# Attention block for one core: x lands transposed by DMA, key maxima scale |Q| in the first head group, and every VectorE exponential takes three VectorE operations

## The chip, the core and the metric

The kernel runs on one core of one Trainium2 chip. A core has TensorE (PE, matrix products into PSUM), VectorE (DVE), ScalarE (ACT), GpSimd (POOL), SyncE (SP, which issues transfers) and 16 DMA engines. The metric is device time in microseconds (us) of one execution; lower is better. The kernel before took 419.52 us (median of three runs, 419.14 to 420.73).

## The reference

One attention block with 16 heads of width 28, for 2048 positions and a model width of 448, in bf16:

```python
qkv = (x @ wqkv).reshape(B, S, 3, H, Dh)            # B=1, S=2048, D=448, H=16, Dh=28
scores = einsum("bhqd,bhkd->bhqk", q, k) * Dh ** -0.5
p = softmax(scores)
o = einsum("bhqk,bhkd->bhqd", p, v)
out = o.reshape(B, S, D) @ wo
```

No score matrix is kept: scores are made tile by tile, exponentiated and multiplied with V at once.

## The kernel before, in words

**Tiles and windows.** The 16 heads form four head groups of four heads. A head is padded from 28 to 32 partitions, so a group's Q or K fills 128. The 2048 queries are four chunks of 512. A window is one head group with one query chunk; there are 16. In a window the keys go by in 16 blocks of 128, so that each window has 16 x 4 = 64 score tiles of 128 keys x 512 queries, 1024 tiles in all. A tile is one matmul (`emit_S`, L652); a row is the four tiles of one key block, and once all four are exponentiated, four matmuls add their products with V to the bank PO (`pv_op`, L816). V has columns of ones, so the softmax denominator comes out beside the product.

**No true maximum is subtracted.** Each head takes 32 more contraction rows beside its own: in Q they hold |Q|, in K a bound made of the largest |K| per dimension (`KMAX`) and a constant mask (`maskm`, -1.03 in data rows, 0 elsewhere). The score matmul over 64 rows thus gives the score less an upper bound. `task_kmax` (L417) makes the bound: four absolute maxima, one per key chunk, are reduced to KMAX, which multiplies the mask; for the first group the first key chunk's rows are written by VectorE (L443) and the others by DMA from `NK` (L438). `task_Q` (L461) makes Q and |Q| (a bitwise AND with 0x7FFF: L491 in the first window, L501 after).

**Two ways to an exponential.** ScalarE takes two tiles at a time from a bank pair PA (one ACTIVATE of 128 x 1024, `try_act`, L955). VectorE takes single tiles from PD or PO by a polynomial on the number's bits (`start_tile`, L735): two linear steps p1 and p2 on VectorE (L757, L760), their product on GpSimd (L763), and a last step f on VectorE that writes the weights PTD (L776). In the kernel before, a tile that starts while GpSimd has little queued goes another way: only p1 on VectorE (L744), then three GpSimd operations (L749, L751, L753), then f. Which tiles go where is decided when the program is built.

**Order.** The order of every engine is fixed at build time by a planner written into the kernel. It keeps a modelled clock, gives each operation a duration, a priority, conditions and banks, and walks forward (the loop at L1000 on). ScalarE pairs come first; a VectorE tile is started when a bank is free; projections of K, Q and V for later groups are tasks with due times. Constants such as J0 (rows that must be ready before a window's first PV), RV, O1 and QEA steer it.

**The start.** Four loads on SP's queue bring x (XS, L208), one more WV (L211); WK and WQ come on ScalarE's queue (L210). Eight matmuls on zeros (L306) run meanwhile. Each block is transposed by 16 TensorE transposes (L322) into PSUM and copied to XT, half by VectorE (L330) and half by ScalarE (L332). XT has 112 contraction rows x 4 pieces. Then come K of the first group (L391), its maxima (L396, L421), K's evictions (L399), Q (L477, L485), |Q| and the bound rows, and the first scores.

**The tail.** The last row groups of the last window are done apart: `finish_window` and the code after the planner's loop copy PO (L684), gather the denominators (`den_gather`, L670; L1090), add the last three rows (L1094), take the reciprocal (L1096), spread it (L1103), scale (L1107), multiply with wo (L1083), add and store (L1112 to L1115).

Of the kernel before, what the change touches and what calls it, by code (L numbers as in the profile page):

```python
# [75 lines left out]
def kernel(  # L76
# [10 lines left out]
    CK = D // CC  # L87
# [18 lines left out]
    J0 = 9  # L106
# [13 lines left out]
    QEA = 20  # L120
# [6 lines left out]
    O1 = 20  # L127
    O2 = 10
    OF = 0.4
    RV = 4  # L130
# [9 lines left out]
    XTH = 1.5  # L140
    PTA1 = 0.6

    x2 = x[0]
    out_perm = out[0].rearrange("(p t) d -> p t d", t=NKT)
    x_perm = x2.rearrange("(p t) c -> p t c", t=NKT)
    wq3 = wqkv.rearrange("(cc p) n -> p cc n", p=CK)

# [7 lines left out]
    XT = [[sb([CK, 2, QW], BF16, f"XT{b}_{hf}") for hf in range(2)] for b in range(NQC)]  # L155
# [19 lines left out]
    DG = DV  # L175
    DW = [sb([P, QW], F16, f"DW{i}") for i in range(2)]
# [21 lines left out]
    OUTF = [sb([P, D], BF16, f"OUTF{i}") for i in range(TPC)]  # L198
# [8 lines left out]
    for b in range(NQC):  # L207
        nc.sync.dma_start(out=XS[b][:], in_=x_perm[:, b * TPC:(b + 1) * TPC, :])  # L208
    for (W, off) in ((WK, D), (WQ, 0)):
        nc.scalar.dma_start(out=W[:, :, 0:GW], in_=wq3[:, :, off:off + GW])  # L210
    nc.sync.dma_start(out=WV[:], in_=wq3[:, :, 2 * D:3 * D])  # L211
# [7 lines left out]

    nc.vector.memset(zeros[:], 0.0)  # L220
# [9 lines left out]
    for i in range(HG):  # L230
        nc.gpsimd.affine_select(out=sel[:, i:i + 1], in_=sel[:, i:i + 1], compare_op=ALU.not_equal,
                                fill=1.0, base=-(HP * i + Dh), pattern=[[0, 1]], channel_multiplier=1)
    nc.gpsimd.memset(ident32[:], 0.0)
    nc.gpsimd.affine_select(out=ident32[:], in_=ident32[:], compare_op=ALU.not_equal,
                            fill=1.0, base=0, pattern=[[-1, P]], channel_multiplier=1)
    for g in range(G):
        for W in (WKP, WQP):
            nc.vector.memset(W[g][:].rearrange("p c (h e) -> p (c h) e", e=HP)[:, :, Dh:HP], 0.0)
    nc.vector.tensor_scalar(out=offscol[:], in0=onescol[:], scalar1=YTOP, scalar2=None, op0=ALU.mult)
# [3 lines left out]
    for g in range(G):  # L243
        nc.vector.memset(VA[g][:].rearrange("p j h e -> p (j h) e")[:, :, Dh:HP], 1.0)
    nc.vector.memset(WO[:], 0.0)
# [55 lines left out]
    xt_half = {}  # L301
# [10 lines left out]
    for b in range(NQC):  # L312
        xs_in = add(Op("SP", 0.01, None, prio=-2000 + b, lat=(4.7, 6.1, 7.6, 9.0)[b]))
        for hf in range(2):
            tv = banks8[2 * b + hf].bitcast(BF16)

            def tr(b=b, hf=hf, tv=tv):
                for c2 in range(2):
                    for t in range(TPC):
                        k = c2 * TPC + t  # L320
                        cc = hf * 2 + c2
                        nc.tensor.transpose(out=tv[0:CK, k * P:(k + 1) * P],  # L322
                                            in_=XS[b][:, t, cc * CK:(cc + 1) * CK], identity=ident[:])
            tro = add(Op("PE", 0.55, tr, deps=[xs_in], prio=-1200 + 10 * b + hf, lat=PLAT, kind="T",
                         acq=(lambda t: not warm_open.__setitem__(0, False)) if (b, hf) == (NQC - 1, 1) else None))

            def ev(b=b, hf=hf, tv=tv):
                i = tv[0:CK, 0:2 * QW].rearrange("p (c q) -> p c q", c=2)
                if hf == 0:
                    nc.vector.tensor_copy(out=XT[b][hf][:], in_=i)  # L330
                else:
                    nc.scalar.copy(out=XT[b][hf][:], in_=i)  # L332
            evo = add(Op("DVE" if hf == 0 else "ACT", 0.6 if hf == 0 else 0.905, ev, deps=[tro], prio=-1200 + 10 * b + hf))
            xt_done[b].append(evo)
            xt_half[2 * b + hf] = evo
# [3 lines left out]
    wkin = add(Op("SP", 0.01, None, prio=-1999, lat=5.1))  # L339
    wqin = add(Op("SP", 0.01, None, prio=-1998, lat=8.3))  # L340
    wvin = add(Op("SP", 0.01, None, prio=-1997, lat=11.0))
# [3 lines left out]
    for g in range(1, G):  # L345
        for (WP, nm, off) in ((WKP, "k", D), (WQP, "q", 0)):
            def ld(g=g, WP=WP, off=off):
                for cc in range(CC):
                    nc.sync.dma_start(
                        out=WP[g][:, cc, :].rearrange("p (h e) -> p h e", e=HP)[:, :, 0:Dh],  # L350
                        in_=wqkv[cc * CK:(cc + 1) * CK, off + g * GW:off + (g + 1) * GW].rearrange("p (h d) -> p h d", d=Dh))
            first = g == 1 and nm == "k"
            w_ready[(nm, g)] = add(Op("SP", 2.4, ld, deps=[xt_done[NQC - 1][0]], prio=-900 if first else g * 256 - 900 + (nm == "q") * 100,
                                      elig=None if first else (lambda t, g=g, nm=nm: pos[0] >= (30 if nm == "q" and g == 1 else (g - 2) * 256 + 120 + 40 * (nm == "q"))), lat=PLT))
# [20 lines left out]
    k0_bank = [(PD[0][:], 0), (PD[2][:], 2), (PO[:], 3), (PA[1][:, QW:2 * QW], 7)]  # L375

    def task_K(g, sc):
        due = g * 4 * WT - 200 + 36 * sc
        if g == 0:
            task = {"slot": None, "ap": k0_bank[sc][0]}  # L380
            acq = lambda t: xt_half[k0_bank[sc][1]].done(t)
# [7 lines left out]
        def ap():  # L389
            return task["ap"] if "ap" in task else bank(task)[:]  # L390
        ops = chain_mm(CC, lambda cc: nc.tensor.matmul(out=ap(), lhsT=WKP[g][:, cc, :], rhs=XT[sc][cc // 2][:, cc % 2, :],  # L391
                                                       start=(cc == 0), stop=(cc == CC - 1)),
                       xt_done[sc] + [w_ready[("k", g)]], prio, elig, acq)
        cs = slice(sc * QW, (sc + 1) * QW)
        if g == 0:
# [3 lines left out]
            evs = [add(Op("ACT", 0.585, lambda pr=pr: nc.scalar.activation(  # L399
                out=KB[0][pr][:, cs], in_=ap(), func=ACT.Identity, bias=onescol[:, 0:1], scale=1.0),  # L400
                deps=[ops[-1], red], prio=prio + 0.1 * pr, lat=0.17,
                acq=(lambda t: quse and quse[0].end is not None) if sc == NQC - 1 else None)) for pr in range(2 if sc == 0 else 1)]
# [14 lines left out]
    def task_kmax(g):  # L417
# [8 lines left out]
        c0 = 1 if g == 0 else 0  # L426
# [716 lines left out]
```

## Time and profile before

| | us |
|---|---|
| the profiled execution's own time | 419.14 |
| its span, first to last instruction | 417.1 |
| median of the runs (419.14 to 420.73) | 419.52 |
| first 1024-column exponential starts | 16.24 |
| last exponential starts | 402.96 |
| last transfers are issued | 414.07 |

The page gives shares by engine and 40 slices of the span; a view by stretches gives each engine's busy time between two moments; a view of waits says who held whom; and the order of time shows single instructions with their start and duration, with the idle time before them and what ended it in brackets. A busy time can be longer than the spacing of instructions, because the end of one overlaps the beginning of the next. "PEld" is TensorE's weight load. The granted TensorE clock is 0.996 of full speed in this run. Of the DMA engines' time, 14.3% went to the queue of most loads.

### The profile page before, as it was taken

The numbers are of one execution on the slowest core, as the hardware profiler recorded it, in microseconds if no ns is written. First come the engines' busy times: TensorE is split into PE (matmuls) and PEld (weight loads), VectorE is DVE, ScalarE is ACT, GpSimd is POOL, SyncE is SP. The second block draws the span as 40 slices with busy tenths as digits, with TensorE's granted clock in tenths as the row PEclk, the third lists the DMA queues.
The fourth block names the chain that finished last, engine by engine and source line by source line (L and its number), as shares of the span: only waits on it lengthen the run. The fifth ranks groups of instructions, "written<-read, shape, count | busy, mean of one in ns | idle before, by whom it ended". The sixth has DMA issues, their size and how long they took to land.

```text
span 417.1 us, 7580 instructions
## 1 busy us (share of the span) xinstructions
PE 363.9 (87%) x2657; PEld 126.1 (30%) x2657; DVE 377.8 (91%) x659; ACT 397.8 (95%) x437; POOL 319.0 (76%) x325
## 2 busy tenths in 40 slices
PE   8989889898988889897988989898888889888996
PEld 5432232222323232322323222322322222222333
DVE  6799999989899999989999999998999899999853
ACT  4999999999999999999999999999999999999961
POOL 3288788797888787798788877888888989787730
PEclk9999999999999999999999999999999999999998
DMA  8410020200401020100401010000311000010112
GB/s 260 73 17 20 3 55 2 48 8 25 100 8 39 1 56 19 29 12 9 114 2 45 3 46 21 7 21 2 96 28 46 2 18 30 9 38 2 70 46 90
DMA packets 33413, 15.84 MB, mean 38 GB/s; under 512 B 26016, under 2 KB 30304, under 8 KB 33376
## 3 DMA queue, kind: packets, MB, share of 16 engines
q1 hardware_dynamic: 32304, 15.05, 14.3%
q8 instruction: 21, 0.34, 0.4%
q10 hardware_dynamic: 1072, 0.32, 0.3%
q14 instruction: 16, 0.13, 0.1%
HBM read 7.37 MB, written 1.96 MB: 22 GB/s over the span
## 4 chain that ended last, share of the span: by engine, by line
ACT 80%; PE 10%; issue 6%; DMA 1%; DVE 1%; SPq 0%; DVEq 0%; ACTq 0%
ACT PTA_132 L955 5%; ACT PTA_131 L955 4%; ACT PTA_133 L955 4%; ACT PTA_136 L955 4%; ACT PTA_137 L955 4%; ACT PTA_140 L955 4%; ACT PTA_138 L955 4%; ACT PTA_134 L955 3%; ACT PTA_139 L955 3%; ACT PTA_141 L955 3%; ACT PTA_142 L955 3%; ACT PTA_143 L955 3%; ACT PTA_135 L955 3%; ACT PTA_144 L955 3%; ACT PTA_145 L955 3%
## 5 line engine op out<-in xcount | busy, mean ns | idle before, releaser
L652 PEld LDWEIGHTS <-KB_1_94 64*128 64x128 bf16 x256 | 21.0, 93 | 50.1 <-issue 48.7
L652 PEld LDWEIGHTS <-KB_1_92 64*128 64x128 bf16 x256 | 20.6, 93 | 47.3 <-issue 44.5
L652 PEld LDWEIGHTS <-KB_0_93 64*128 64x128 bf16 x256 | 20.2, 93 | 43.4 <-issue 41.9
L652 PEld LDWEIGHTS <-KB_0_91 64*128 64x128 bf16 x256 | 19.9, 93 | 40.6 <-issue 37.6
L763 POOL TENSOR_TENSOR DV_180<-DV_180,DU_174 128x512 f16<-128x512 f16 x24 | 27.7, 1153 | 4.5 <-DVE DV_180 L760 3.7
L763 POOL TENSOR_TENSOR DV_177<-DV_177,DU_171 128x512 f16<-128x512 f16 x24 | 27.7, 1155 | 4.0 <-DVE DV_177 L760 3.6
L763 POOL TENSOR_TENSOR DV_179<-DV_179,DU_173 128x512 f16<-128x512 f16 x21 | 24.2, 1155 | 5.6 <-DVE DV_179 L760 4.9
L763 POOL TENSOR_TENSOR DV_176<-DV_176,DU_170 128x512 f16<-128x512 f16 x21 | 24.2, 1154 | 2.1 <-DVE DV_176 L760 1.0
L763 POOL TENSOR_TENSOR DV_175<-DV_175,DU_169 128x512 f16<-128x512 f16 x18 | 20.8, 1153 | 4.0 <-DVE DV_175 L760 3.5
L763 POOL TENSOR_TENSOR DV_178<-DV_178,DU_172 128x512 f16<-128x512 f16 x18 | 20.8, 1155 | 3.2 <-DVE DV_178 L760 2.8
L955 ACT ACTIVATE PTA_139<-PA_195 128x1024 bf16<-128x1024 f32 x18 | 22.4, 1246 | 0.0
L955 ACT ACTIVATE PTA_140<-PA_196 128x1024 bf16<-128x1024 f32 x18 | 22.2, 1233 | 0.2 <-PE PO L816 0.2
L955 ACT ACTIVATE PTA_141<-PA_195 128x1024 bf16<-128x1024 f32 x18 | 22.2, 1236 | 0.0
L955 ACT ACTIVATE PTA_142<-PA_196 128x1024 bf16<-128x1024 f32 x17 | 21.3, 1252 | 0.0
L955 ACT ACTIVATE PTA_138<-PA_196 128x1024 bf16<-128x1024 f32 x17 | 21.1, 1240 | 0.0
L955 ACT ACTIVATE PTA_143<-PA_195 128x1024 bf16<-128x1024 f32 x16 | 20.1, 1254 | 0.0
L955 ACT ACTIVATE PTA_137<-PA_195 128x1024 bf16<-128x1024 f32 x16 | 19.7, 1232 | 0.0
L955 ACT ACTIVATE PTA_136<-PA_196 128x1024 bf16<-128x1024 f32 x15 | 18.5, 1231 | 0.0
L757 DVE TENSOR_SCALAR DU_171<-PD_199 128x512 f16<-128x512 uint16 x24 | 16.4, 683 | 1.7 <-PE PD_199 L652 1.4
L760 DVE SCALAR_TENSOR_TENSOR DV_177<-PD_199,DU_171 128x512 f16<-128x512 uint16 x24 | 16.4, 683 | 0.3
L757 DVE TENSOR_SCALAR DU_174<-PD_199 128x512 f16<-128x512 uint16 x23 | 15.7, 681 | 1.0 <-PE PD_199 L652 0.9
L955 ACT ACTIVATE PTA_146<-PA_196 128x1024 bf16<-128x1024 f32 x13 | 16.4, 1260 | 0.0
(656 smaller groups left out, 1665.8 us busy)
## 6 DMA issues: line engine op xcount, KB each, us to landing
RRB_191<-SCR_193 SPq DMA_DIRECT2D x8, 256.0 KB
RRB_192<-SCR_194 SPq DMA_DIRECT2D x7, 256.0 KB
KB_1_94<-KB_0_93 SPq DMA_DIRECT2D x4, 128.0 KB
XS_127<-in_x_dram SPq DMA_DIRECT2D x1, 448.0 KB
XS_128<-in_x_dram SPq DMA_DIRECT2D x1, 448.0 KB
XS_129<-in_x_dram SPq DMA_DIRECT2D x1, 448.0 KB
XS_130<-in_x_dram SPq DMA_DIRECT2D x1, 448.0 KB
out_dram<-XS_127 SPq DMA_DIRECT2D x1, 448.0 KB
```

The costliest lines, as they stand in the source:

```text
L652: nc.tensor.matmul(out=ap, lhsT=KB[g % 2][i // 2][a:a + 64, j * P:(j + 1) * P], rhs=QB[w % NQB][i // 2][a:a + 64, :], start=True, stop=Tru ...
L757: p1 = add(Op("DVE", P1, lambda: nc.vector.tensor_scalar(out=DU[b][:], in0=lo, scalar1=SIG / 65536, scalar2=SIG * (SS - 0.5), op0=ALU.mult ...
L760: p2 = add(Op("DVE", P1, lambda: nc.vector.scalar_tensor_tensor(out=DV[b][:], in0=lo, scalar=65536 * (SS - 0.5 + CE / C3), in1=DU[b][:], o ...
L763: gq = add(Op("POOL", PTT, lambda: nc.gpsimd.tensor_tensor(out=DG[b][:], in0=DV[b][:], in1=DU[b][:], op=ALU.mult), deps=[p2], prio=n, kind ...
L955: nc.scalar.activation(out=PTA[pslot.idx][:, 0:len(ns) * QW], in_=PA[s.idx][:, 0:len(ns) * QW], func=ACT.Exp, bias=ACT_BIAS, scale=ACT_SCALE)
```

## The change

1. x is no longer loaded as it is and transposed by TensorE. Eight transposing DMAs on ScalarE's queue (two for each block of 512 positions: columns 0 to 383, and the last 128 columns) write XT as 128 contraction rows x 4 pieces. The fourth piece begins at column 320, so 64 of its rows repeat columns that piece three has; the weights of those rows are set to zero (`DUP`). XT's copies and the 64 TensorE transposes are gone. WK, WQ and WV come on SP's queue, each in two loads. The planner's assumed landing times change with it (`XLAND`, `WLAND`).
2. In the first head group the roles of bound and |Q| change places: |Q| is multiplied by KMAX, and K's bound rows are the constant mask, which doesn't wait for the maxima. The first two key chunks' rows are written by GpSimd, the others by DMA from `maskm`. In the first window one of the four |Q| parts is made by ScalarE (Abs with a scale), the others by AND and multiply on VectorE; in the group's later windows GpSimd multiplies. K's third and fourth evictions go from ScalarE to VectorE.
3. The tile way with one step on VectorE and three on GpSimd is gone: each VectorE tile takes p1, p2 and f. GpSimd's product gets a tile of its own (`DG`) in place of writing over `DV`.
4. The position of x's rows in a block is by stretches of 128 rather than interleaved by 16, in the loads and in the output. Some memsets move to GpSimd. J0, QEA, O1 and RV get other values, and the banks of the first projections are assigned anew.

The lists of instructions of the two programs: 1024 score tiles are 843 for ScalarE and 181 for VectorE before (126 with two first steps on VectorE, 55 with one), 848 and 176 after. VectorE has 661 instructions before and 700 after, GpSimd 330 and 231. In the list after, the waits of the transposing loads show that loads share eight completion counters in turn, so that later loads are issued only when the counter's earlier one has landed: the second load of block two waits for WK's first load, block three for WK's second and WQ's first, block four for block one's second and WQ's second.

```diff
-    J0 = 9
+    J0 = 10
...
-    QEA = 20
+    QEA = 30
...
-    O1 = 20
+    O1 = 30
...
-    RV = 4
+    RV = 2
...
+    XLAND = (4.9, 6.6, 8.4, 10.2)
+    WLAND = (4.9, 5.5, 10.5)
...
-        nc.sync.dma_start(out=XS[b][:], in_=x_perm[:, b * TPC:(b + 1) * TPC, :])
-    for (W, off) in ((WK, D), (WQ, 0)):
-        nc.scalar.dma_start(out=W[:, :, 0:GW], in_=wq3[:, :, off:off + GW])
-    nc.sync.dma_start(out=WV[:], in_=wq3[:, :, 2 * D:3 * D])
...
+            nc.scalar.dma_start_transpose(out=XT[b][:, 0:CC - 1, :], in_=xb[:, 0:(CC - 1) * P])
+            nc.scalar.dma_start_transpose(out=XT[b][:, CC - 1:CC, :], in_=xb[:, CS[CC - 1]:D])
+    for (W, off, n) in ((WK, D, GW), (WQ, 0, GW), (WV, 2 * D, D)):
+        for ps, cs, i in w_chunks(off, n):
+            nc.sync.dma_start(out=W[ps, cs, 0:n], in_=i)
...
+    for W in (WK, WQ, WV):
+        nc.vector.memset(W[0:DUP, CC - 1, :], 0.0)
...
-        xs_in = add(Op("SP", 0.01, None, prio=-2000 + b, lat=(4.7, 6.1, 7.6, 9.0)[b]))
+        xs_in = add(Op("SP", 0.01, None, prio=-2000 + b, lat=XLAND[b]))
+        if b not in PEB:
+            xt_done[b].append(xs_in)
+            continue
...
-                kmrep[(g, 0, i)] = add(Op("DVE", 0.36, (lambda i=i, st=st: nc.vector.tensor_scalar(
-                    out=KB[0][i // 2][HP * st:HP * (st + 1), 0:QW], in0=maskm[HP * SI[i]:HP * (SI[i] + 1), :],
-                    scalar1=KMAX[g][HP * SI[i]:HP * (SI[i] + 1), 0:1], scalar2=None, op0=ALU.mult)),
...
+                for c in range(KD):
+                    kmrep[(g, c, i)] = add(Op("POOL", 0.6, (lambda i=i, st=st, c=c: nc.gpsimd.tensor_scalar(
+                        out=KB[0][i // 2][HP * st:HP * (st + 1), c * QW:(c + 1) * QW], in0=maskm[HP * st:HP * (st + 1), :],
+                        scalar1=1.0, scalar2=0.0, op0=ALU.mult, op1=ALU.add)), deps=[kev[(0, c, i)]], prio=-900 + i + 4 * c))
...
+                if i == 1:
+                    o = add(Op("ACT", 0.5, lambda o_=o_, i_=i_, k_=k_: nc.scalar.activation(out=o_, in_=i_, func=ACT.Abs, scale=k_),
+                               deps=[e0, kmax_op[0]], prio=-1090))
...
+                    o = add(Op("DVE", 0.33, lambda o_=o_, k_=k_: nc.vector.tensor_scalar(
+                        out=o_, in0=o_, scalar1=k_, scalar2=None, op0=ALU.mult), deps=[ab, kmax_op[0]], prio=-939 + 0.01 * i))
...
+        if g == 0:
+            ab = add(Op("POOL", PTS, lambda: nc.gpsimd.tensor_scalar(
+                out=QP[n][:], in0=QP[n][:], scalar1=KMAX[g][:, 0:1], scalar2=None, op0=ALU.mult),
+                deps=[ab, kmax_op[0]], prio=-10, kind="n"))
...
-        two = pool_load(t) < XTH and x_busy[0] < t
-        if two:
-            p1 = add(Op("DVE", P1, lambda: nc.vector.tensor_scalar(
...
-            ga = add(Op("POOL", PTA1, lambda: nc.gpsimd.tensor_scalar(
...
-            gb_ = add(Op("POOL", PTT, lambda: nc.gpsimd.tensor_tensor(out=DV[b][:], in0=DU[b][:], in1=DU[b][:], op=ALU.mult),
...
-            gq = add(Op("POOL", PTT, lambda: nc.gpsimd.tensor_tensor(out=DG[b][:], in0=DV[b][:], in1=wb[:], op=ALU.mult),
```

## The prediction, made before the changed kernel was run

> **What bounds the kernel now.** I read the page's shares first, then its 40 slices, then ScalarE's waits, then stretches of the span, and last both ends in order of time. From the page:
>
> ```profile
> PE 363.9 (87%) x2657; PEld 126.1 (30%) x2657; DVE 377.8 (91%) x659; ACT 397.8 (95%) x437; POOL 319.0 (76%) x325
> ...
> ACT  4999999999999999999999999999999999999961
> ```
>
> ScalarE (ACT) is filled in every slice but the first and the last two. Busy times by stretch (columns: stretch, length, then each engine's busy time with its count):
>
> ```profile
> 208.00:256.00 48.00, 41.88 (x303) 13.51 (x295) 46.39 (x81) 48.00 (x54) 38.28 (x37) 1.00 0.09 24
> 16.24:403.60 387.36, 340.48 (x2466) 112.26 (x2464) 361.10 (x613) 386.87 (x422) 315.02 (x306) 1.00 0.13 31
> 403.60:417.10 13.50, 8.78 (x93) 5.72 (x89) 5.54 (x12) 1.37 (x3) 0.00 (x0) 0.87 0.20 69
> ```
>
> From 16.24 to 403.60 ScalarE is busy 386.87 of 387.36 us: a gapless stream of 422 exponentials (421 of 1024 columns, one of 512). So the time is four terms: first exponential at 16.24, the stream, a tail of 13.5, and 2.04 around the span (419.14 - 417.10, the profiled execution's own time). The sum is made against 419.14; the median, 419.52, is 0.4 higher. About 0.5% (2.1 us) is what a measurement of this kernel can tell from no change.
>
> VectorE (DVE) matters second: busy 361.10 of 387.36 in the stream, 46.39 of 48 in one stage, and there ScalarE still lost nothing.
>
> **The stream.** By the two programs' instruction lists, 1024 score tiles divide into 843 for ScalarE and 181 for VectorE before, 848 and 176 after. That is 424 exponentials of 1024 columns. Spacing: from 17.50 (the second) to 402.96 (the last) there are 420 steps, 385.46 us, 0.918 each. Before: 16.24 to 403.59 = 387.35. After: 423 x 0.918 + 1.03 for the last + 0.2 that the second waits for VectorE's extra operations = 389.5. **+2.2.**
>
> VectorE's tiles cost more. Before, 126 take three VectorE operations and 55 take two (488); after, 176 x 3 = 528. GpSimd goes from 126 + 55 x 3 operations to 176, so nothing of its part can be late: it sheds 55 x (0.62 + 1.04 + 1.15) = 155 us and gains 50 x 1.155 = 58. A VectorE operation is shown as 0.68 but the next starts 0.60 on:
>
> ```profile
> 204.95 0.68 DVE L776 SCALAR_TENSOR_TENSOR PTD_158<-PD_197,DV_178 128x512 uint16<-128x512 f32 x1
> 205.55 0.68 DVE L776 SCALAR_TENSOR_TENSOR PTD_159<-PD_198,DV_179 128x512 uint16<-128x512 f32 x1
> ```
>
> So 40 x 0.60 = 24.0 more, and two key evictions that ScalarE did (2 x 0.65): 361.1 + 25.3 = 386.4 of a stream of 389.5. The old busy time counts an overlapping 0.08 before each gap; by spacing alone its operations add up to about 353, so after about 378, 97%. Cover is nearly gone. Bounds for what ScalarE then loses: nothing, as in the stage at 46.39 of 48; or, if VectorE keeps the 26 us that it now idles, 386.4 + 26.3 - 389.5 = 23. I take 0.8, near the lower end: the stage at 97% is the closest row, and the exponentials are ordered so that VectorE gets fewer tiles.
>
> **The start.** The order of time, old kernel (start, duration):
>
> ```profile
> 9.29 0.61 PE L322 MATMUL PA_195<-ident,XS_130 128*112 128x128 bf16 x8
> ...
> 12.22 0.59 PE L391 MATMUL PA_196<-XT_0_69,WKP_79 112*128 112x512 bf16 x2
> ...
> 13.36 0.69 DVE L396 TENSOR_REDUCE KPART_95<-PA_196 128x1 f32<-128x512 f32 x1 [0.17 <-PE PA_196 L391]
> 14.08 0.16 DVE L421 TENSOR_REDUCE KMAX_99<-KPART_95 128x1 f32<-128x4 f32 x1
> 14.28 0.72 DVE L443 TENSOR_SCALAR KB_0_91<-maskm,KMAX_99 32x512 bf16<-32x512 bf16 x2
> 15.03 0.60 DVE L491 TENSOR_SCALAR QB_0_85<-QB_0_85 32x512 uint16<-32x512 uint16 x2
> 15.78 0.39 PE L652 MATMUL PA_195<-QB_0_85,KB_0_91 64*128 64x512 bf16 x2
> ```
>
> The last x block is there at 9.07 (its first weight load). Then come 64 transposes' last 16, their evictions on VectorE and ScalarE, the key projection, four maxima, bound rows, |Q|. Transposes and evictions go: 9.07 to 12.22, 3.15 us. After the key maximum the old chain has 0.72 of bound rows and 0.60 of |Q|; in their place stand one multiply on VectorE (0.36, half of L443's pair) and beside it one scaled Abs on ScalarE. That form is not in the trace; between 0.30 (half of L491) and 0.69 (ScalarE's 128x512 eviction) I take 0.69, its own engine. The chain from the landing: four matmuls and their end 12.22 to 13.36 = 1.14; reduction 0.72; maximum 0.20; Abs with its wait 0.10 + 0.69; last score matmul to exponential 0.25 + 0.15 = **3.25** in all. Old: 7.17.
>
> When does the last block land? No row shows a transposing load. Lower bound: as a plain load, 9.07. Upper: each byte holds the DMA engines twice as long; the blocks filled them from about 2.6 to 9.07, so 15.5. Two things speak for more than 9.07. By the list's waits, loads share eight completion counters: the last block's two transposing loads may issue only once the first block's second part and the second part of WQ are there, and WQ was waited for until 8.08 before. And ScalarE's queue holds eight issues ahead of its table load (1.28) and its evictions. The planner in the diff assumes 10.2; of its old assumptions (4.7, 6.1, 7.6, 9.0) the trace shows 4.6, 6.2, 7.85, 9.07. I take 10.4, nearer to the plain load. First exponential: 10.4 + 3.25 = 13.65, **-2.6**. Per us of later landing, +1.
>
> The Trainium skill ("DMA: Bandwidth & Descriptors", Latency and other measured facts) gives a transposing DMA an effective 261 GB/s, or 350-400 when contiguous. This trace moved plain blocks 1.5 us apart (448 KB, about 300 GB/s) and shows no transposing one. An estimate from the page: 1.835 MB at 261 is 7.0 us, 2.0 + 7.0 + 1.6 for the weights = 10.6, and the sum 0.2 higher.
>
> A second rule speaks against the change. The fillers stand 0.43 apart early (3.57 for eight), later matmuls 0.215 (0.86 for four). The skill ("TensorE: Matmul & The Clock Gate", What's actually happening) says the slow clock is the default and comes back after an idle window of about 3.4 us. Without transposes TensorE waits for landings; if it fell slow, the last four matmuls would cost 0.86 more.
>
> Hidden at no cost: memsets moved to GpSimd (VA 0.27 each on VectorE; GpSimd waited 4.39 us for WQ there), constant bound rows (8 GpSimd operations, 0.62 each by L749's row for the same operation on more partitions, and four copies on SP's queue, needed from tile 16 and 32, some 6 and 12 us later), three Q multiplies on GpSimd (0.62 each, 24 us ahead of use). If this cover went, the first windows would wait 1 to 2 us.
>
> **The tail.** Old kernel, last exponential to end:
>
> ```profile
> 402.96 0.63 ACT L955 ACTIVATE PTA_143<-PA_196 128x512 bf16<-128x512 f32 x1
> ...
> 403.85 0.69 DVE L684 COPY OSB_186<-PO 128x512 f32<-128x512 f32 x1 [2.26 <-PE PO L816]
> ...
> 405.13 1.06 PE L670 MATMUL PD_199<-sel,OSB_186 128*128 128x4 f32 x8 [0.65 <-DVE XS_129 L622]
> ...
> 408.25 0.26 DVE L1096 RECIPROCAL RT<-PD_199 128x16 f32<-128x16 f32 x1 [2.11 <-PE PD_199 L1090]
> ```
>
> After its last score matmul (402.23) the old TensorE still had 20 PV matmuls; then copy, additions, the denominators (L670), three rows of L1090 and L1094 (0.82 each), done at 408.7, 5.1 after the last exponential. In the new list all PV but the last three rows stand ahead of the third last score pair, some 3.6 us before the last exponential ends, and L670's matmuls between the last pairs. The old chain from PV's end to 408.7 takes 4.9, so it would end 1.3 to 2.0 after the exponential. Gain between 0 (VectorE, now full, copies late) and 3.7; I take 3.1, nearest to the list's order. Tail 10.4, **-3.1**.
>
> **Sum.** 13.65 + 389.5 + 0.8 + 10.4 + 2.04 = **416.4**, 0.65% under 419.14.
>
> **Rivals.**
> - *VectorE becomes the bound* (the other side). Place: the score stream, where a PV row waits for its VectorE tiles and TensorE, in order, holds back the next score pair. From VectorE waits of about 11 us (389.5 less 378) on, each us is one. If it keeps 19 to 24 of its idle, ScalarE loses 8 to 13: 424 to 429. For: 97%. Against: 96.6% in one stage without loss. Chance 0.16.
> - *Transposing loads are slow.* Last landing at 12 to 15.5: 418 to 421.5. For: the shared counters. Against: bytes are the same. 0.15.
> - *The tail gives nothing* because VectorE is behind at the end: 419.5. 0.08.
> - *The change does less than it says*: blocks land as plain loads would (9.07), and nothing is lost: 414 to 415. 0.06.
> - Forecast, 415 to 417.4: 0.55.
>
> Faster by over 0.5% (under 417.4): forecast, the last rival, a little of the slow loads: 0.62. Within: 0.21. Slower: 0.17, the first rival. Range 413.2 to 421.4: from the earliest landing with the full tail gain to the latest landing; left out is the first rival.
>
> **What would show it.** First exponential at 13 to 15; 424 exponentials of 0.918 with under 2 us of idle; VectorE busy 97-99% of the stream; denominators' reciprocal within 3 us of the last exponential. Wrong if ScalarE waits for score matmuls in mid-stream, or the first exponential is past 16.

## The result: 424.3 us, 1.1% slower, and the whole miss lies before the first exponential

The changed kernel takes 424.34 us (median of four runs, 423.56 to 424.57) beside 419.33 for the kernel before on the same chip (418.52 to 420.73): a ratio of 1.0113, with a 95% interval of 1.0082 to 1.0143 (further down intervals stand in brackets behind the ratio to the kernel before, which ran again beside every run). The forecast was 416.4 with 421.4 as its upper end.

The profiled execution took 424.49, its span is 422.6. From the page after (engines' shares, ScalarE's row of slices, two DMA queues with packets, MB and share of 16 engines; q10 is ScalarE's queue):

```profile
PE 366.6 (87%) x2612; PEld 122.1 (29%) x2612; DVE 393.6 (93%) x698; ACT 396.1 (94%) x435; POOL 237.2 (56%) x226
...
ACT  0499899999999999999999999999999999999991
...
q1 hardware_dynamic: 32576, 13.22, 13.3%
q10 hardware_dynamic: 8592, 2.21, 3.1%
```

ScalarE's first slice went from 4 to 0, its second from 9 to 4; the last but one went from 6 to 9. The view by stretches, cut at the first and last exponential (length, busy times of PE, PEld, DVE, ACT and POOL with counts, granted clock, DMA share, GB/s):

```profile
22.22:412.48 390.26, 347.81 (x2520) 114.03 (x2519) 381.42 (x657) 389.10 (x424) 225.77 (x194) 1.00 0.13 30
412.48:422.60 10.12, 6.15 (x62) 3.87 (x58) 3.83 (x10) 1.37 (x4) 0.00 (x0) 0.83 0.26 91
```

| term | before | forecast | after | after less forecast |
|---|---|---|---|---|
| last x block is there | 9.07 | 10.4 | 18.12 | +7.7 |
| from there to the first exponential | 7.17 | 3.25 | 4.10 | +0.85 |
| stream | 387.36 | 390.3 | 390.26 | 0 |
| tail | 13.50 | 10.4 | 10.12 | -0.3 |
| around the span | 2.04 | 2.04 | 1.89 | -0.15 |

Three of five terms came out to 0.3 us, over 390 us of stream. The start is 8.6 us off. In order of time, ScalarE's queue of the changed kernel (start, duration):

```profile
0.71 1.40 ACTq L226 DMA_TRANSPOSE XT_63<-in_x_dram  x1
...
3.45 2.18 ACTq L226 DMA_TRANSPOSE XT_64<-in_x_dram  x1
5.67 1.52 ACTq L227 DMA_TRANSPOSE XT_64<-in_x_dram  x1
...
11.75 1.68 ACTq L227 DMA_TRANSPOSE XT_66<-in_x_dram  x1
13.46 1.28 ACT L235 ACT_TABLE_LOAD   x1 [13.46 <-DMA XT_65<-in_x_dram]
...
22.22 1.02 ACT L994 ACTIVATE PTA_127<-PA_195 128x1024 bf16<-128x1024 f32 x1 [0.46 <-PE PA_195 L709]
```

Each transposing load holds the queue for 1.28 to 2.18 us, eight of them until 13.43. The plain loads of x before held SP's queue for 0.38 to 0.52 each. TensorE and the chain to the first exponential:

```profile
12.20 0.81 PE L418 MATMUL PO<-XT_65,WKP_75 128*128 128x512 bf16 x3 [1.23 <-DMA XT_65<-in_x_dram]
13.82 0.38 PE L418 MATMUL PO<-XT_65,WKP_75 128*128 128x512 bf16 x1 [0.81 <-DMA XT_65<-in_x_dram]
18.17 1.87 PE L418 MATMUL PD_198<-XT_66,WKP_75 128*128 128x512 bf16 x4 [3.97 <-DMA XT_66<-in_x_dram]
```

The chain of waits has one piece here, "9.96 8.16 DMA XT_66<-in_x_dram": from the issue of block four's first load to its landing. The four products that follow take 1.87 where the forecast's chain had them at a full clock; the clock granted from 18 to 20 us is 0.50. DMA engines are over-full all the while, and a view of the transfers alone, 0 to 20 us, says with what:

```profile
q10 hardware_dynamic: 8448, 2.10, 63.2%
q1 hardware_dynamic: 2104, 1.14, 32.7%
```

63.2% of 20 us is 12.6 us of all 16 engines for 2.10 MB of x, and 32.7% is 6.5 us for 1.14 MB of weights, wo and constant rows. Together 19.1 us. The view by stretches has the engines at a share of 1.19 (last number but one; packets of one engine overlap, so it can be over 1):

```profile
2.00:18.00 16.00, 8.20 (x24) 2.69 (x23) 5.26 (x18) 4.52 (x7) 7.48 (x19) 0.88 1.19 199
```

So 19.1 us of packets fill the 16.1 us from 2 to 18.1, where block four lands. This only adds up what the trace holds; what the parts are worth, runs 2 to 5 show.

### The profile page after: what moved, and what is told of

Read it like the earlier page. It is cut to its first block, busy times and chain, and to the rows that moved or that the text cites. A ratio compares the mean times of both kernels' runs of the same rounds, so it can differ in the third digit from the quotient of the medians.

```text
span 422.6 us, 7570 instructions
## 1 busy us (share of the span) xinstructions
PE 366.6 (87%) x2612; PEld 122.1 (29%) x2612; DVE 393.6 (93%) x698; ACT 396.1 (94%) x435; POOL 237.2 (56%) x226
## 4 chain that ended last, share of the span: by engine, by line
ACT 83%; issue 6%; PE 5%; ACTq 2%; DMA 2%; DVE 0%
ACT PTA_127 L994 4%; ACT PTA_129 L994 4%; ACT PTA_128 L994 4%; ACT PTA_131 L994 4%; ACT PTA_132 L994 4%; ACT PTA_130 L994 4%; ACT PTA_137 L994 4%; ACT PTA_133 L994 4%; ACT PTA_136 L994 4%; ACT PTA_135 L994 4%; ACT PTA_134 L994 4%; ACT PTA_139 L994 3%; ACT PTA_141 L994 3%; ACT PTA_138 L994 3%; ACT PTA_145 L994 3%
## 5 line engine op out<-in xcount | busy, mean ns | idle before, releaser
L805 POOL TENSOR_TENSOR DG_177<-DV_171,DU_165 128x512 f16<-128x512 f16 x30 | 34.7, 1155 | 29.5 <-DVE DV_171 L802 29.4
L805 POOL TENSOR_TENSOR DG_178<-DV_172,DU_166 128x512 f16<-128x512 f16 x30 | 34.6, 1155 | 29.1 <-DVE DV_172 L802 28.9
L805 POOL TENSOR_TENSOR DG_181<-DV_175,DU_169 128x512 f16<-128x512 f16 x29 | 33.5, 1155 | 29.0 <-DVE DV_175 L802 28.2
L805 POOL TENSOR_TENSOR DG_180<-DV_174,DU_168 128x512 f16<-128x512 f16 x29 | 33.5, 1154 | 26.3 <-DVE DV_174 L802 25.8
L805 POOL TENSOR_TENSOR DG_179<-DV_173,DU_167 128x512 f16<-128x512 f16 x29 | 33.5, 1155 | 21.1 <-DVE DV_173 L802 20.9
L805 POOL TENSOR_TENSOR DG_182<-DV_176,DU_170 128x512 f16<-128x512 f16 x29 | 33.5, 1156 | 20.9 <-DVE DV_176 L802 20.7
L994 ACT ACTIVATE PTA_141<-PA_195 128x1024 bf16<-128x1024 f32 x18 | 22.6, 1258 | 0.0
L994 ACT ACTIVATE PTA_140<-PA_196 128x1024 bf16<-128x1024 f32 x18 | 22.6, 1254 | 0.0
L994 ACT ACTIVATE PTA_139<-PA_195 128x1024 bf16<-128x1024 f32 x18 | 22.5, 1251 | 0.0
L994 ACT ACTIVATE PTA_138<-PA_196 128x1024 bf16<-128x1024 f32 x18 | 22.5, 1249 | 0.0
L994 ACT ACTIVATE PTA_136<-PA_196 128x1024 bf16<-128x1024 f32 x18 | 22.4, 1247 | 0.0
L994 ACT ACTIVATE PTA_137<-PA_195 128x1024 bf16<-128x1024 f32 x18 | 22.4, 1246 | 0.0
L994 ACT ACTIVATE PTA_135<-PA_195 128x1024 bf16<-128x1024 f32 x18 | 22.4, 1246 | 0.0
L994 ACT ACTIVATE PTA_134<-PA_196 128x1024 bf16<-128x1024 f32 x18 | 22.4, 1242 | 0.0
L799 DVE TENSOR_SCALAR DU_168<-PD_197 128x512 f16<-128x512 uint16 x29 | 19.7, 679 | 0.8 <-PE PD_197 L709 0.8
L799 DVE TENSOR_SCALAR DU_167<-PD_199 128x512 f16<-128x512 uint16 x29 | 19.7, 681 | 0.7 <-PE PD_199 L709 0.5
L799 DVE TENSOR_SCALAR DU_165<-PD_197 128x512 f16<-128x512 uint16 x29 | 19.7, 681 | 0.6 <-PE PD_197 L709 0.5
L802 DVE SCALAR_TENSOR_TENSOR DV_174<-PD_197,DU_168 128x512 f16<-128x512 uint16 x29 | 19.7, 681 | 0.2
```

The costliest lines, as they stand in the source:

```text
L799: p1 = add(Op("DVE", P1, lambda: nc.vector.tensor_scalar(out=DU[b][:], in0=lo, scalar1=SIG / 65536, scalar2=SIG * (SS - 0.5), op0=ALU.mult ...
L802: p2 = add(Op("DVE", P1, lambda: nc.vector.scalar_tensor_tensor(out=DV[b][:], in0=lo, scalar=65536 * (SS - 0.5 + CE / C3), in1=DU[b][:], o ...
L805: gq = add(Op("POOL", PTT, lambda: nc.gpsimd.tensor_tensor(out=DG[b][:], in0=DV[b][:], in1=DU[b][:], op=ALU.mult), deps=[p2], prio=n, kind ...
L994: nc.scalar.activation(out=PTA[pslot.idx][:, 0:len(ns) * QW], in_=PA[s.idx][:, 0:len(ns) * QW], func=ACT.Exp, bias=ACT_BIAS, scale=ACT_SCALE)
```

## The experiments

Theory A: the loss is the landing of transposed x, and the other parts are worth what was forecast. The rivals are in the texts on record.

**1. All blocks by TensorE (e1).**

```diff
-    PEB = ()
-    XLAND = (4.9, 6.6, 8.4, 10.2)
+    PEB = (0, 1, 2, 3)
+    XLAND = (4.7, 6.1, 7.6, 9.0)
```

(and banks for the four added transposes)

> The changed kernel with part 1 undone: all four x blocks come by plain loads on SP's queue and TensorE transposes them; the other parts stay. Theory A (only the late landing of the transposing loads costs; stream and tail are as predicted): last block at about 9.1, transposes and copies 3.2, then 3.3 to 4.1 to the first exponential, so 15.5 to 16.5 in place of 22.2; stream 390.3, tail 10.2, 1.9 around: 418 to 419. Rival B (the 40 more VectorE operations cost the time): the stream loses in any case, 422 or more. Rival C (ScalarE's queue, not the landing): same first exponential as A.

Measured: 423.17, ratio 1.0092 [1.0061, 1.0123], first exponential at 21.89. The time lies in rival B's range, but not by B's cause, for the stream takes 390.6 as in the changed kernel. Theory A missed by an effect of the undoing itself:

```profile
10.15 0.28 DVE L320 COPY WKP<-WK 128x448 bf16<-128x448 bf16 x1 [5.30 <-DMA WK<-in_wqkv_dram]
10.34 0.68 DVE L358 COPY XT<-PA 128x1024 bf16<-128x1024 bf16 x1
```

WK now stands on SP's queue behind all of x. VectorE waits 5.30 us for it, and the copies of x's transposes, long ready, queue behind that one copy. The weights' queue belongs to part 1, and this run didn't undo it; run 6 does.

**2. Transposing loads on SP's queue, weights on ScalarE's (e2).**

```diff
-            nc.scalar.dma_start_transpose(out=XT[b][:, 0:CC - 1, :], ...
+            nc.sync.dma_start_transpose(out=XT[b][:, 0:CC - 1, :], ...
...
-            nc.sync.dma_start(out=W[ps, cs, 0:n], in_=i)
+            nc.scalar.dma_start(out=W[ps, cs, 0:n], in_=i)
```

> The eight transposing loads are issued by SP, the weights' loads by ScalarE. Theory A (landing): the first exponential stays at 21 to 23 and the time at 423 to 425. Rival C (ScalarE is held by 12.7 us of issues, then its table load and six evictions up to 18.3, and that sets the start): ScalarE is free from 3 us on, the first exponential comes 2 to 6 us earlier, 418 to 422.

Measured: 420.32 (one run), first exponential at 17.80: rival C's range. But the landing moved too, which C did not say. The issues are no faster (1.23 to 2.14 each, the last ends at 13.11), yet block four's products start at 14.54, 3.6 us earlier:

```profile
11.85 1.26 SPq L227 DMA_TRANSPOSE XT<-in_x_dram  x1
13.22 1.80 SPq L270 DMA_DIRECT2D WO<-in_wo_dram  x4
```

```profile
14.54 1.06 PE L418 MATMUL PD<-XT,WKP 128*128 128x512 bf16 x4 [0.92 <-DMA XT<-in_x_dram]
```

WO is issued behind x and no longer shares the engines with it; as x's queue changed as well, run 4 has to separate the two. TensorE runs at its full clock (1.00 from 14 to 15 us; four products 1.06), and the chain from them to the first exponential takes 3.26: the forecast's 3.25 was right for a TensorE at full clock.

**3. A third of the bytes in each block's first load (e3), and two issues in place of eight (e4).** e3 loads 128 columns for 384, and the middle pieces of XT are constants; e4 loads all 2048 rows at once.

```diff
-            nc.scalar.dma_start_transpose(out=XT[b][:, 0:CC - 1, :], in_=xb[:, 0:(CC - 1) * P])
+            nc.scalar.dma_start_transpose(out=XT[b][:, 0:1, :], in_=xb[:, 0:P])
```

> Still eight transposing loads, but each block's first brings 128 columns in place of 384 (half of the transposed bytes); the two middle pieces of XT are set to a constant, so that much of x is left out. Theory A1 (the DMA engines' time on the transposed bytes sets the landing): 13 us of the 16 engines become some 6.5, the last landing falls from 18.1 to 12 to 14, the first exponential to 16 to 18. Rival A2 (the count of issues, 1.3 to 2.2 us each, sets it): last landing stays at 17 to 18.

```diff
-    for b in range(NQC):
+    for k in range(1):
...
+        nc.scalar.dma_start_transpose(out=XTA[k][:, 0:CC - 1, :], in_=xb[:, 0:(CC - 1) * P])
```

> The same transposed bytes in two loads of 2048 rows in place of eight of 512 rows. Theory A1 (engine time on the bytes): the data are all there at 15 to 18, no block earlier. Rival A2 (count of issues): all there by 8 to 10, the first exponential below 15 and the time at 417 or less.

Measured: e3 422.47, e4 427.56 (one run each). With half the bytes each issue still takes 1.24 to 1.40 and the eighth ends at 11.32, though the engines' time on that queue is halved (1.5% of the span for 3.1%). With two issues the queue is held as long:

```profile
0.71 7.93 ACTq L224 DMA_TRANSPOSE XTA<-in_x_dram  x1
8.67 4.49 ACTq L225 DMA_TRANSPOSE XTA<-in_x_dram  x1
13.18 1.28 ACT L233 ACT_TABLE_LOAD   x1 [13.18 <-issue]
```

In both, the last piece of x lands some 3 us earlier than in the changed kernel:

```profile
15.05 0.38 PE L420 MATMUL PD<-XT,WKP 128*128 128x512 bf16 x1 [0.86 <-DMA XT<-in_x_dram]
```

```profile
15.22 0.59 PE L416 MATMUL PA<-XTA,WKP 128*128 128x512 bf16 x1 [0.34 <-DMA XTA<-in_x_dram]
```

e3 (15.05, first exponential 18.03) stands between its two theories. e4 has the same bytes and lands at 15.22, as A1 said, and A2 falls; there WO is issued at 13.48, behind x as in run 2, and the time is long because no block is there before 13.44 (first exponential 22.50). So there are two floors of about the same height: the queue (some 1.3 us for 512 rows however few the columns, about 12.5 us for all of x) and the engines (12.6 us). Neither fewer issues nor fewer bytes alone moves x to 9 us.

**4. WV and WO out of x's way (f1).**

```diff
-    for (W, off, n) in ((WK, D, GW), (WQ, 0, GW), (WV, 2 * D, D)):
+    for (W, off, n) in ((WK, D, GW), (WQ, 0, GW)):
...
+    for ps, cs, i in w_chunks(2 * D, D):
+        nc.scalar.dma_start(out=WV[ps, cs, 0:D], in_=i)
...
+    add(Op("SP", 2.4, ld_wo, prio=-800, elig=at(160), lat=6.0))
```

> The changed kernel with two loads taken out of the way of the transposing loads: WV's two loads follow the transposing loads on ScalarE's queue, and WO's four are issued late in the stream; nothing else is changed but what the plan makes of it. Theory D (the last block lands late because other loads' packets share the 16 DMA engines with it; with the weights' issue on SP and nothing behind it, it landed at about 14.5): the last block's first product is at 14.3 to 15.3 instead of 18.17, the first exponential at 18 to 19, total 420.0 to 421.3. Theory E (ScalarE's queue itself is slow at transposing loads; SP's queue is the better one): the last block is still there only at 17 to 18.5, first exponential 21 to 22.5, total 423 to 425.

Measured: 430.56, ratio 1.0278 [1.0250, 1.0305]. On the landing theory D is right and E falls: block four's products start at 14.09 on ScalarE's queue too. WO is the load that runs 2 and 4 both took out of x's way.

```profile
14.09 1.02 PE L421 MATMUL PD<-XT,WKP 128*128 128x512 bf16 x4 [1.01 <-DMA XT<-in_x_dram]
18.22 1.87 PE L952 MATMUL PD<-zrow,zeros 128*128 128x512 bf16 x4 [3.11 <-ACT QB L527]
```

On the time both miss, D by 9 us, because the edit made new waits. ScalarE's first eviction stands behind ten issues and the table load (15.17), Q's comes at 16.89. |Q| waits for that one, and VectorE's last reduction queues behind |Q|, 3 us after its products:

```profile
17.62 0.53 DVE L540 TENSOR_SCALAR QB<-QB 32x512 uint16<-32x512 uint16 x1 [3.82 <-ACT QB L527]
18.18 0.69 DVE L426 TENSOR_REDUCE KPART<-PD 128x1 f32<-128x512 f32 x1
```

First exponential: 20.69. In run 2, with block four as early and ScalarE free of the issues, it was 17.80: the queue that rival C named costs up to 2.9 us once the landing no longer hides it. TensorE, idle 3.11 us, then runs at half clock (0.50 from 18 to 24), and ScalarE waits before each of the next pairs. WO's late issues on SP at 82.86 hold up Q's copies, and one exponential comes 2.20 late at 99.07:

```profile
22.70 2.06 ACT L997 ACTIVATE PTA<-PA 128x1024 bf16<-128x1024 f32 x2 [0.98 <-PE PA L712]
25.18 1.02 ACT L997 ACTIVATE PTA<-PA 128x1024 bf16<-128x1024 f32 x1 [0.42 <-PE PA L712]
...
99.07 13.86 ACT L997 ACTIVATE PTA<-PA 128x1024 bf16<-128x1024 f32 x15 [2.20 <-PE PA L712]
```

The stream takes 395.0 for 390.3, the tail 11.8.

**5. Plain loads in the transposing loads' place (g1).** Same bytes, tiles and queue:

```diff
-            nc.scalar.dma_start_transpose(out=XT[b][:, 0:CC - 1, :], in_=xb[:, 0:(CC - 1) * P])
-            nc.scalar.dma_start_transpose(out=XT[b][:, CC - 1:CC, :], in_=xb[:, CS[CC - 1]:D])
+            xf = xb.rearrange("(p t) d -> p (t d)", t=TPC)
+            nc.scalar.dma_start(out=XT[b][:, 0:CC - 1, :].rearrange("p c q -> p (c q)"), in_=xf[:, 0:(CC - 1) * QW])
+            nc.scalar.dma_start(out=XT[b][:, CC - 1, :], in_=xf[:, TPC * D - QW:TPC * D])
```

> The changed kernel with its eight transposing loads replaced by eight plain loads of the same bytes (2.10 MB, into the same tiles, on the same queue and with the same waits after them); x is then not transposed, so this run leaves out that part of the computation. Nothing else is changed. Theory A (how long the transposing loads take is the whole error): last block there at 9 to 11, first exponential at 12.5 to 14.5, stream and tail as in the changed kernel (390.3 and 10.1), total 415 to 417.5. Rival F (the weights on SP, the eight issues ahead of ScalarE's evictions, or a slow TensorE clock would hold the start up even so): first exponential after 16, total over 418.5.

Measured: 418.10, ratio 0.9966 [0.9948, 0.9984], between the two theories. Transfers of the first 16 us, and the last x pieces:

```profile
q10 hardware_dynamic: 1152, 2.10, 40.0%
q1 hardware_dynamic: 2104, 1.14, 28.0%
```

```profile
11.42 0.81 PE L419 MATMUL PD<-XT,WKP 128*128 128x512 bf16 x3 [0.73 <-DMA XT<-in_x_dram]
12.82 0.38 PE L419 MATMUL PD<-XT,WKP 128*128 128x512 bf16 x1 [0.59 <-DMA XT<-in_x_dram]
```

The first exponential comes at 15.39, 6.8 us earlier than in the changed kernel, with nothing changed but the kind of load. 40.0% of 16 us is 6.4 us for the same 2.10 MB that took 12.6 transposed. Engine time also depends on what else is in flight: with WO behind them (run 2, first 14.5 us) the transposed bytes took 73.1%, 10.6 us,

```profile
q1 hardware_dynamic: 8449, 2.11, 73.1%
```

and the 1.14 MB of other loads took 4.5 us here (28.0%) for 6.5 beside transposing loads. So transposing takes 1.7 to 2.0 times the engine time of plain loads. But plain loads of this layout, with the weights on SP beside them, also land only at 12.8, not at 9 to 11. So 7.7 us of late landing divide into 5.3 (18.1 - 12.8) for transposing and 2.4 (12.8 - 10.4) that any load in this arrangement would pay: 14% more bytes of x, 1.14 MB of other loads in the same stretch, and issues held until an earlier load has landed (the fourth on ScalarE's queue stands until 4.19). Which of these makes the 2.4 was not tried. Nor is the 5.3 a fixed price: with WV and WO out of the way, transposed x landed at 14.09 (run 4), 1.3 later than the plain loads here.

**6. TensorE transposes with the weights where they were (f2).** As run 1, and WK and WQ on ScalarE's queue:

```diff
-            nc.sync.dma_start(out=W[ps, cs, 0:n], in_=i)
+            (nc.sync if n == D else nc.scalar).dma_start(out=W[ps, cs, 0:n], in_=i)
```

> Part 1 undone with the weights where they were before: all four x blocks come as plain loads on SP and are transposed by TensorE, WK and WQ come on ScalarE's queue, WV on SP behind x. Parts 2, 3 and 4 of the change stay. Theory A (the whole loss is the start, and there the landing of transposed x; bound rows that are constants, three VectorE steps, the new constants and the tail are each worth what was forecast): the first exponential is at 14.8 to 16.2, no later than the 16.24 of before, and the time is 416.3 to 418.3, under before. Rival (the gain of the tail or the three-step tiles needs the new start, or the bound rows gain nothing): 418.5 to 421.

Measured: 419.53, ratio 1.0019 [1.0003, 1.0036]. The landing's loss is gone, but so is the gain: the rival's range. First exponential 16.82, second 18.50 (before: 16.24, 17.50), tail 10.6.

**7. Two blocks transposed by DMA (f3), one block (g4).** f3: blocks one and two plain on SP, three and four transposing on ScalarE's queue. g4: run 6 with block four by two transposing loads on SP behind the plain ones.

```diff
-    PEB = ()
+    PEB = (0, 1)
```

> Blocks one and two of x as plain loads on SP (each followed by WK's, then WQ's loads) and TensorE transposes, blocks three and four by four transposing loads on ScalarE's queue; parts 2, 3 and 4 stay. If the issue of transposing loads (1.3 to 2.2 us each) sets the landing: the four are issued by 6.5, the last block is there at 8 to 10.5 and the first exponential is at 12.5 to 15; total 414.5 to 417. If instead the bytes of transposing loads set it (2.21 MB took 13.1 us of all engines; half of that, 6.5 us, beside 1.2 MB of plain loads at 320 GB/s, 3.7 us): last landing 10.5 to 12, first exponential 14.5 to 16, total 416.5 to 418.5. If plain and transposing loads hinder each other: first exponential after 17, total over 419.

```diff
-    PEB = (0, 1, 2, 3)
+    PEB = (0, 1, 2)
...
-            nc.scalar.dma_start_transpose(out=XT[b][:, 0:CC - 1, :], ...
+            nc.sync.dma_start_transpose(out=XT[b][:, 0:CC - 1, :], ...
```

> The version with all four blocks transposed by TensorE and weights on ScalarE's queue (419.5), but with block four alone by two transposing loads, issued by SP behind the three plain x loads. Theory A with the measured terms (two issues of 1.3 after the plain ones, 0.55 MB at some 170 GB/s behind the plain loads): block four is there at 10.5 to 12 in place of the 14 at which its evicted transposes were; first exponential at 15 to 16 in place of 16.82, second with no gap; total 417 to 418.8. If transposing and plain loads hinder each other as in the mixed version (a plain x block that came 3 us late): first exponential over 16.8, total 419.5 to 421.5.

Measured: f3 423.48, ratio 1.0115 [1.0086, 1.0144]. The third case held: the plain block two came at 9.18 beside the transposing loads (6.2 in the kernel before, where its issue ended 1.4 us earlier, at 1.58 for 3.02), the fourth issue took 3.21, the table load (8.91) and both copies of x on ScalarE (from 10.21) started behind it, and the first exponential came at 19.13.

g4 423.37, ratio 1.0090 [1.0070, 1.0111]. Its first exponential is where theory A said (15.87), the earliest of all versions that transpose x, though the two issues took 2.38 and 2.93 and the second exponential came 0.8 late (17.68). The gain is lost again further on, and theory A's total with it: TensorE's clock is 0.50 from 20 to 24 us, pairs come late there and the stream takes 392.7; and its plan leaves 88 matmuls behind the last exponential (62 in the changed kernel), the reciprocal comes 4.35 after it (1.6), and the tail is 14.3:

```profile
15.87:408.61 392.74, 349.43 (x2497) 113.61 (x2495) 381.85 (x655) 389.52 (x424) 225.34 (x195) 0.99 0.13 30
408.61:422.90 14.29, 9.34 (x88) 5.83 (x86) 5.23 (x12) 1.37 (x3) 0.00 (x0) 0.71 0.18 65
```

**8. Part 3 out of the changed kernel (f4), and part 3 alone in the kernel before (g2).** f4 puts the two-way tile back; g2 takes it out of the old kernel (GpSimd's product still writes over DV there).

```diff
+        two = pool_load(t) < XTH and x_busy[0] < t
+        if two:
```

> The changed kernel with the two-way VectorE tile put back (one VectorE step and three GpSimd steps when GpSimd has little queued, as before); x still lands transposed. If part 3 is worth what was forecast (VectorE full costs 0.8 us over the stream, and the plan with three-step tiles takes five tiles fewer on VectorE): 423.5 to 425.5, no more than 1 us from the changed kernel's 424.3. If three-step tiles cost the stream more than forecast: 420.5 to 423. If they are a gain of their own (less GpSimd work beside VectorE): 425.5 to 428.

```diff
-        two = pool_load(t) < XTH and x_busy[0] < t
-        if two:
```

> Part 3 alone: the kernel before with three VectorE operations for every VectorE tile; start, bound rows and constants stay. If part 3 costs only what the count of ScalarE's exponentials says (424 for 422, two tiles fewer for VectorE in each pair: +2.2 us) and VectorE at 97% costs 0.8, and the tail's gain is not part 3's: 421.5 to 423. If the shorter tail (3 us) comes with the three-step tiles: 418.5 to 420.5.

Measured: f4 430.98, ratio 1.0286 [1.0257, 1.0315]; g2 417.11, ratio 0.9937 [0.9912, 0.9961]. f4 lies beyond the third case expected of it and g2 below its second: part 3 is a gain, in either surrounding. g2 by stretches:

```profile
16.43:405.85 389.42, 345.06 (x2499) 112.70 (x2498) 381.13 (x656) 389.06 (x424) 221.17 (x191) 1.00 0.13 31
405.85:415.40 9.55, 5.34 (x79) 3.48 (x77) 3.90 (x10) 1.37 (x3) 0.00 (x0) 1.00 0.28 98
```

The stream pays 2.06 for three-step tiles (2.2 forecast), with VectorE busy 97.9% and ScalarE idle for 0.36 us in all. The tail gives back 3.95, of which 1.45 lie behind the reciprocal, where the work is the same and the clock is not (last section). f4 has a tail of 14.6 and a stream of 392.0 for two exponentials fewer.

**9. The four constants alone (g3), and with part 3 (h1).**

```diff
-    J0 = 9
+    J0 = 10
-    QEA = 20
+    QEA = 30
-    O1 = 20
+    O1 = 30
-    RV = 4
+    RV = 2
```

> Part 4's four planner constants alone: the kernel before with J0 10, QEA 30, O1 30 and RV 2; tiles, start and bound rows stay. If the shorter tail comes with the constants (the plan then puts the last PV matmuls before the last score pairs, with 423 exponentials in place of 422): 416 to 418. If the tail's gain needs the three-step tiles, as the changed kernel with two-way tiles (tail 14.6) suggests: 419 to 421.

> Parts 3 and 4's constants together on the kernel before: three VectorE operations for every VectorE tile and J0 10, QEA 30, O1 30, RV 2; x, its transposes and the bound rows stay. Beside the version with parts 2, 3 and 4 and no part 1 (419.5, first two exponentials at 16.82 and 18.50), this leaves out only part 2, the 128-row pieces and the order of x's rows. If part 2 is worth nothing at the start or costs (two more VectorE operations between the maximum and the second exponential): first two at 16.2 to 16.5 and 17.5 to 17.8, total 416 to 418. If part 2 gains and the 419.5 comes from parts 3 and 4 together: 419 to 421.

Measured: g3 416.39, ratio 0.9926 [0.9901, 0.9950]; h1 416.96, ratio 0.9941 [0.9917, 0.9964]. Both times are in the first case's range (h1's first two exponentials, at 16.04 and 17.30, even 0.2 earlier than it said), and with g2 these three are faster than either kernel; their intervals overlap, so no order among them is shown. Parts 3 and 4's constants do not add up: each alone brings the reciprocal to within 2.2 or 2.3 us of the last exponential, both to 1.6. Against the kernel before on its own chip h1 is 2.6 us faster (419.52); f2, which has part 2 and the new layout besides, is 0.6 slower (418.96). Between the two profiles (spans of 414.2 and 418.4; h1's execution was 1.0 faster than its median, f2's 0.7 slower) stand 0.8 of start, 1.7 of stream and 1.7 of tail (the last goes with the clock, below):

```profile
16.04:405.25 389.21, 344.98 (x2508) 113.73 (x2517) 380.24 (x657) 388.98 (x424) 221.29 (x191) 1.00 0.13 31
405.25:414.20 8.95, 4.77 (x62) 2.98 (x58) 3.74 (x10) 1.37 (x4) 0.00 (x0) 1.00 0.30 104
```

```profile
16.82:407.78 390.96, 347.96 (x2520) 114.26 (x2518) 382.20 (x658) 389.14 (x424) 225.79 (x195) 1.00 0.12 30
407.78:418.40 10.62, 6.43 (x62) 4.12 (x58) 3.76 (x10) 1.37 (x3) 0.00 (x0) 0.76 0.25 88
```

## Why the prediction was wrong, point by point

- **The landing, the step that failed.** The last x block was forecast at 10.4 and came at 18.12. "Upper: each byte holds the DMA engines twice as long [...] so 15.5" doubled the old stretch from 2.6 to 9.07, and that held too little:

```profile
2.60:9.07 6.47, 6.23 (x58) 3.91 (x56) 4.75 (x12) 2.50 (x4) 2.00 (x7) 1.00 1.05 352
```

  By this row the engines worked 6.8 us there (1.05 of 6.47), on x's 1.84 MB and about 0.5 MB of other loads; doubled, 13.6. In the changed kernel they worked 19.1 us by 18.1: 12.6 on x, which has 14% more bytes (2.10 MB; "bytes are the same" and the 1.835 MB of the estimate leave out the columns that are loaded twice), and 6.5 on 1.14 MB of other loads. The factor two had no row behind it, but came out about right (1.7 to 2.0, run 5). The choice of 10.4, "nearer to the plain load", had no row behind it either: it rested on the planner's assumption, written into the code, and on plain blocks. Even plain loads in this arrangement land at 12.8 (run 5).
- **"ScalarE's queue holds eight issues"** was named, at no price. Each took 1.28 to 2.18 us, and that queue also carries the table load and the evictions. Here it wasn't the last wait, since block four came later still; in run 4 it was.
- **The chain, 3.25.** Measured 4.10, and 3.26 with TensorE at full clock (run 2). The excess is mostly the four last products: 1.90 to the reduction for 1.14, at a clock of 0.50. That case was priced in the text at 0.86, for the clock rule of the Trainium skill ("TensorE: Matmul & The Clock Gate", What's actually happening), and left out of the sum. It came with the late landing: in run 5, where x landed piece by piece until 12.82, the clock was 1.00 throughout. The trace has the slow clock (0.53 from 14 to 16 us, 0.50 from 16 to 20) but not that rule's condition, an idle window of about 3.4 us before it: the clock fell at 14.2, as the 3.97 us without work began, and from 1.60 until then no wait of TensorE had been longer than 1.4 us.
- **Part 2.** From the start of the maximum to the first exponential: 2.16 before (14.08 to 16.24), 1.43 after (20.79 to 22.22), as forecast. In run 6 it was 1.51, but the maximum came 1.2 later there than before (15.31 for 14.08), and the second exponential waits for two more multiplies. Which of the new layout, the split weight loads and the order of evictions makes the maximum late wasn't taken apart. On this kernel parts 1, 2 and the layout together gain nothing.
- **The stream, 390.3.** Right to 0.1. Of the 0.8 allowed for a full VectorE, 1.16 us of idle were seen after the first exponential, but in one place, 46.2 to 48.4 us, where TensorE does PV matmuls of many rows between two score pairs. VectorE at 97.9% of the stream cost nothing in g2. So the first rival fell, and that the allowance had about the right size is luck: what it was meant for cost nothing. VectorE's busy time was 381.42, 5 less than the 386.4 that was added up.
- **The tail, 10.4.** Right, 10.12: the reciprocal is 1.63 after the last exponential ("1.3 to 2.0"). That the sum is within 0.3 is partly luck, since the 8.49 us behind the reciprocal go with the clock, by up to 2.4 us between the runs shown in the last section.
- **The rivals.** "Transposing loads are slow: 418 to 421.5" had the mechanism, at 0.15 and with a bound that was too low. It was this one that ended slower than before, not VectorE.

The Trainium skill ("DMA: Bandwidth & Descriptors", Latency and other measured facts) gave 261 GB/s and, with it, an estimate of 10.6. Here 2.10 MB in 12.6 us of all engines are 167 GB/s (198 with the 10.6 us of run 2), and from the first issue to the last landing (17.4 us) it is 121. A second page ("Advanced Engine Details and Errata", X-Bar Transpose (TRN2)) says that transposing transfers are as fast as regular ones; the changed kernel and run 2, beside run 5, show 1.7 to 2.0 times the engine time. The measurement decides.

## What to carry to other kernels

Before a load is moved into another form, add up the engine time of everything that is in flight in the same stretch, with the new form at its worst bound, and see which queue each issue holds and who stands behind it: here 12.6 + 6.5 us of transfers and 12.5 us of issue replaced 3.15 us of transposes and copies. The terms that were forecast on a profile's rows (stream, tail, and the chain at full clock) came out; the one that rested on a constant in the code did not. A term without a row should be put at the middle of its bounds at least (12.3 here), and the bounds themselves be added up from everything in flight: 15.5 was still 2.6 short. And undo a change part by part: the parts that pay here (three-step tiles or four planner constants, 416.4 to 417.1) are not the one that the change is named for.

## What the runs showed of the hardware that was not expected

- A transposing load of 512 rows holds the issuing queue 1.23 to 2.18 us where all of x comes so, with little difference between 128 and 384 columns, and up to 3.21 beside plain loads of x (run 7); for 2048 rows it is 4.49 and 7.93 us (128 and 384 columns). A plain load of the same bytes holds it 0.33 to 0.45 (run 5).
- The granted clock of TensorE is not the same in each execution, and part of the tail goes with it. The last 22 matmuls, between reciprocal and end, are the same work in these three:

```profile
408.25:417.10 8.85, 4.79 (x22) 2.90 (x18) 3.25 (x8) 1.37 (x3) 0.00 (x0) 0.81 0.17 54
```

```profile
406.80:416.60 9.80, 5.86 (x22) 3.17 (x18) 3.27 (x8) 1.37 (x3) 0.00 (x0) 0.67 0.22 75
```

```profile
408.00:415.40 7.40, 3.19 (x22) 1.84 (x18) 3.18 (x8) 1.37 (x3) 0.00 (x0) 1.00 0.28 97
```

The kernel before (clock 0.81) takes 8.85, g3 (0.67) 9.80, g2 (1.00) 7.40. So 2.4 us of tail go with the clock, as much as most parts of this change are worth. Executions of one kernel differ likewise: of the seventeen of the kernel before beside g2 and g3, the two at a mean clock of 1.000 took 417.8 and 418.4, the others (0.990 to 0.996) 419.2 to 420.6. All four of g2 ran at 0.998 or more, so at an equal clock its gain is nearer to 1.0 than to 2.6; g3 and h1 gain 2.4 and 2.2 in such executions (h1 against a single one, 418.5). What sets the clock there was not tried.
